# Pairing two heads' products with v on the column halves of the array, constant products at the start, and FFN steps 1.2 tiles apart

## The chip, the cores and the metric

The kernel runs on one core of a Trainium2 chip. The time is that of one execution on the device, in microseconds (us); lower is better. The engines are called TensorE (PE in the profile, with its weight loads as PEld), VectorE (DVE), ScalarE (ACT), GpSimd (POOL) and SyncE (SP, which starts the DMAs). 0.5% of this kernel's time is about 7 us.

## The reference, cut to what matters

Attention over 8 batches of 8 heads with a threshold in the softmax, and behind it a feed-forward net (FFN) over all 4608 rows:

```python
scores = scale * np.matmul(q, k.transpose(0, 1, 3, 2))          # (8, 8, 576, 576), head_dim 64
thresh = np.max(scores, axis=-1, keepdims=True) - tau
scores = np.where(scores >= thresh, scores, -1000000000.0)
scores = scores - np.max(scores, axis=-1, keepdims=True)
attn = np.exp(scores)
attn = attn / (np.sum(attn, axis=-1, keepdims=True) + 1e-09)
attn_out = np.matmul(attn, v)
...
x = attn_out.transpose(0, 2, 1, 3).reshape(4608, 512)
h = x @ w_in                                                    # 512 -> 2048
r = np.maximum(h, 0.0)
g = s * (r * r) + b
return g @ w_out                                                # 2048 -> 512
```

## The kernel before

**Tiles.** A tile is 128 queries of one head (the 64 queries left over, the tail, of two heads share a tile). For each tile (`tile_of`) PE multiplies q with k (L328, 576 scores a query in two halves of 288), DVE copies the scores out with their maximum (L331), ACT takes the exponential (L337), DVE applies the threshold and sums (L340), GpSimd divides (L348), PE transposes the weights in five pieces (L357, L358), ACT copies them out of PSUM, and PE multiplies them with v.

**The unsplit batch.** Batch 0 (`Plain`, 36 tiles) works in plain float32. Its products with v stand at L373: five for a tile (four over 128 keys and one over the last 64), each with v of 64 columns as the stationary side, so that they fill half of the array's columns. The profile counts each as two records. The transposed weights lie in `e32(i)`, one of two buffers that alternate from tile to tile; L364 and L365 copy into it, L373 reads it, and L376 copies the result out of the PSUM bank `pv` into x. A visit is one pair of heads and 256 queries; its tiles come as head 0 (two tiles, and a tail tile in some visits), then head 1 (two tiles). Batches 1 to 7 split every operand into two parts that TensorE takes faster (`Head`, L404), and their order is not touched.

**The FFN** (`Block`) works on 256 rows at a time, in 16 steps over the hidden columns: 12 products into `h` (L535), ACT and GpSimd in between, six products into `o` (L548). Before its first step a block's input is split (`stage`: ACT L518 to xh, DVE L520 to xl). Weights of step f are loaded and split on the way, in `weights`. 18 blocks of 16 steps stand against 288 tiles.

**What sets the order.** `Plan` takes every operation with its engine, cost in ns, dependencies and due time `at` (in tiles), simulates the engines and hands out the least due of what is ready. The program is then emitted in this order, and each engine works through its own queue in order. A block's step f falls due at `when + each * f`; `when` is the end of the block before, or 1.5 tiles after the tile that completes the input, whichever is later. `each` is 1.125 tiles in the first half, so that 16 steps take 18 tiles, which is the distance of two blocks.

**The start.** The first scores wait for q and k of the first pair. GpSimd fills the constants meanwhile (L673 and around it), among them `ones` (L671) and the zeros `qt` (L670).

Of the kernel before, what the change touches and what calls it, by code (L numbers as in the profile page):

```python
# [9 lines left out]
F32 = mybir.dt.float32  # L10
# [10 lines left out]
SCORES_AHEAD, VALUES_AFTER = 1, 1  # L21
FFN_AFTER = 1.5


TWO_BANKS = 16
WEIGHTS_AT, WEIGHTS_EACH = 12, 1.5
# [80 lines left out]
def tile_attention_ffn(ctx: ExitStack, tc: tile.TileContext, qT, kT, v, tau, w_in, w_out, s, b, out):  # L107
# [73 lines left out]
    def pe(n, cols, fn, r, w, at):  # L181

        plan.add("PE", (n * (0.452 * cols + 1.5), n * (0.452 * cols + 1.5) + 170), fn, r, w, at)

# [130 lines left out]
    def tile_of(ti, i):  # L315
# [4 lines left out]
        sm_k, em_k, get = buffers(i)  # L320
        plain = ti.plain

        def scores():
            for hf in range(2):
                cs = slice(hf * HS, (hf + 1) * HS)
                seq = ti.st()
                for n, (stat, kk) in enumerate(seq):
                    nc.tensor.matmul(ps[:, hf, 0:HS], stat, kk[:, cs], start=(n == 0), stop=(n == len(seq) - 1))  # L328
        pe(2 if plain else 4 * len(ti.heads), HS * (3.7 if plain else 1), scores, ti.kq(), [bk], i - SCORES_AHEAD)

# [28 lines left out]
        pe(4.3, 240, transposes, [em_k, "ident"], ["tp", "tt"], i + 0.5)  # L359
        if plain:  # L360
            ke = ("e32", i % 2)

            def both():
                nc.scalar.copy(out=e32(i)[:, 0:NQ], in_=tp)  # L364
                nc.scalar.copy(out=e32(i)[0:T, NQ], in_=tt)  # L365
            act((660, 760), both, ["tp", "tt"], [ke], i + 0.5)
            for pr, j, cs, dest, key in plain:
                n = cs.stop - cs.start

                def products(pr=pr, j=j, cs=cs, n=n):  # L370
                    for kt in range(5):
                        ks = slice(0, P if kt < NQ else T)
                        nc.tensor.matmul(bank["pv"][0:D, 0:n], pr.get()[2][ks, j, kt], e32(i)[ks, kt, cs], start=(kt == 0),  # L373
                                         stop=(kt == 4))
                pe(5, n * 4, products, [ke, pr.keys[2 + j], pr.keys[2 + j] + (1,)], ["pv"], i + VALUES_AFTER)
                act((80 + 0.75 * n, 180 + 0.75 * n), lambda dest=dest, j=j, n=n: nc.scalar.copy(  # L376
                    out=dest[j * D:(j + 1) * D], in_=bank["pv"][0:D, 0:n]), ["pv"], [key], i + VALUES_AFTER)
            return
# [210 lines left out]
    def make_tiles(vis, A, Bh):  # L589
# [7 lines left out]
        if A is Bh:  # L597
            for j in range(2):
                for i in range(2):
                    ti = Tile_()  # L600
                    c, r = t0 * P + i * P, slice(j * D, (j + 1) * D)
                    ti.st = lambda c=c, r=r: [(A.get()[1][r, c:c + P], A.get()[0][r])]
                    ti.kq = lambda: A.keys[:2]
                    ti.plain = [(A, j, fl, xb[xk][:, pair, i * P:(i + 1) * P], ("x", xk, pair, j, i))]
                    ti.heads, ti.blocks = [A], []
                    tiles.append(ti)
                if tail and not j:
# [3 lines left out]
                    ti.plain = [(A, u_, slice(u_ * T, (u_ + 1) * T), xtl, ("xt", bi % 4, pair, u_)) for u_ in range(2)]  # L611
# [50 lines left out]
    n_plain = sum(ti.plain is not None for ti in tiles)  # L662


    pairs[0].load(-30)
    dma(0.5, lambda: nc.sync.dma_start(out=tau_t, in_=tau.partition_broadcast(P)), [], ["tau"], -20)

    def constants():
        make_identity(nc, ident)
        nc.gpsimd.memset(qt.bitcast(F32), 0.0)  # L670
        nc.gpsimd.memset(ones.bitcast(F32), 1.0)  # L671
# [5 lines left out]
    pool((1500, 1500), constants, [], ["ident", "ones", "qd0", "qd1", "qt0", "qt1", "sm0", "sm1", "em0", "em1"], -9)  # L677
    for ap, t, k in (s, s_t, "s_"), (b, b_t, "b"):
# [24 lines left out]
    for i, ti in enumerate(tiles):  # L703
        ti.tag = "o" if i < TWO_BANKS and i % 2 else "s"

        events.append((i, lambda ti=ti, i=i: tile_of(ti, i)))
        for g in () if ti.plain else ti.end:
            events.append((i + 0.1, lambda g=g, i=i: with_v(g, i + VALUES_AFTER)))
        if True:
            for k_ in ti.blocks:  # L710
                when = max(when, i + FFN_AFTER)
                each = 1.125 if i < len(tiles) // 2 else 1.0

# [60 lines left out]
```

## Time and profile before

| | |
|---|---|
| median of 3 runs | 1428.97 us (1423.86 to 1429.4) |
| the profiled execution | 1427.36 us |
| its span, first to last instruction | 1425.4 us |
| mean granted clock of TensorE | 0.994 |
| first product of the first FFN block (L535) | 77.10 us after the span's start |
| first product of the second FFN block | 195.31 us |

A row of the timeline reads: start in us, length in us (of all instructions merged into the row), engine, line, operation, output <- inputs, partitions x columns of the stationary side, shape, count. A row of the groups gives count, busy us, mean ns, and the idle time ahead with what ended it. Matmuls overlap in the pipeline, so the distance of two starts says more than a length.

### The profile page before, as it was taken

The page shows a single profiled execution, that of the slowest core. Times are in us where ns is not written, and L with a number is a line of the kernel's source. Part 1 is how long each engine was busy: PE and PEld are TensorE (multiplying, and loading weights), DVE is VectorE, ACT ScalarE, POOL GpSimd, SP SyncE. Part 2 cuts the span into 40 slices and gives each one's busy share as a digit, 9 for nine tenths or more (in the row PEclk, how much of TensorE's full clock was granted, in tenths as well). Part 3 has the DMA queues.
Part 4 walks back from the last instruction along what each step waited for, and adds up shares of the span by engine and source line. Part 5 has one row for each costly group of instructions (what it writes and reads, how often), then busy time and mean ns, then how long its engine had stood idle before and what let it go on. Part 6 is the DMA issues. An engine that isn't in the chain of part 4 may idle for free.

```text
span 1425.4 us, 29320 instructions
## 1 busy us (share of the span) xinstructions
PE 1392.9 (98%) x9328; PEld 1255.2 (88%) x9328; DVE 1074.0 (75%) x3099; ACT 991.4 (70%) x2487; POOL 730.5 (51%) x798
## 2 busy tenths in 40 slices
PE   8999999999999999999999999999999999999998
PEld 5677789898898989898999999999999999999887
DVE  4877777988888887988789887888788787886101
ACT  3777667777777767777677777776777777776443
POOL 1223345656565556656566556665556556653210
PEclk9999999999999999999999999999999999999999
DMA  8610011322222221322222222222222222220000
GB/s 294 246 39 21 23 58 52 95 58 61 60 79 73 59 79 52 95 59 62 64 66 80 70 72 65 80 65 63 63 75 69 76 57 70 61 85 1 16 16 15
DMA packets 94539, 99.58 MB, mean 70 GB/s; under 512 B 34480, under 2 KB 72368, under 8 KB 94384
## 3 DMA queue, kind: packets, MB, share of 16 engines
q1 hardware_dynamic: 94384, 97.71, 23.1%
q8 instruction: 73, 1.20, 0.3%
q14 instruction: 82, 0.67, 0.1%
HBM read 88.21 MB, written 9.44 MB: 69 GB/s over the span
## 4 chain that ended last, share of the span: by engine, by line
PE 92%; DVE 5%; issue 1%; ACT 1%; POOL 0%; DMA 0%; DVEq 0%; SPq 0%; ACTq 0%; POOLq 0%
PE h L535 28%; PE o L548 27%; PE s L328 12%; PE tp L357 9%; PE pv L404 9%; PE pv L373 4%; PE tt L358 2%; DVE em L340 1%; DVE e L391 1%; PE o L328 1%; PE h L487 1%; DVE xl L520 1%; DVE oo L559 0%; DVE e L393 0%; DVE x L411 0%
## 5 line engine op out<-in xcount | busy, mean ns | idle before, releaser
L535 PE MATMUL h<-xh,w 128*128 128x256 f32 x2304 | 471.1, 287 | 2.8 <-ACT xh L518 1.7
L535 PEld LDWEIGHTS h<-xh,w 128*128 128x128 f32 x2304 | 380.9, 192 | 13.0 <-ACT g L538 3.3
L348 POOL TENSOR_SCALAR em<-em,st 128x576 f32<-128x576 f32 x288 | 251.8, 874 | 272.6 <-DVE st L345 116.5
L548 PE MATMUL o<-w,gh 128*128 128x512 f32 x1152 | 370.0, 402 | 0.9 <-ACT g L538 0.5
L542 POOL TENSOR_TENSOR gl<-g,gh 128x256 fp32r<-128x256 f32 x272 | 213.2, 784 | 276.6 <-ACT gh L541 117.7
L535 PE MATMUL h<-xl,w 128*128 128x256 f32 x1152 | 328.8, 285 | 7.3 <-DVE xl L520 7.3
L340 DVE SCALAR_TENSOR_TENSOR em<-sm,st,em 128x577 f32<-128x577 f32 x288 | 253.0, 878 | 42.1 <-ACT em L337 32.0
L331 DVE TENSOR_SCALAR_CACHE_REDUCE sm<-s 128x576 f32<-128x576 f32 x280 | 211.2, 754 | 94.3 <-PE s L328 91.8
L337 ACT ACTIVATE em<-sm,st 128x576 f32<-128x576 f32 x288 | 224.9, 781 | 33.6 <-DVE sm L331 32.6
L538 ACT ACTIVATE g<-h 128x256 f32<-128x256 f32 x288 | 109.3, 380 | 194.9 <-PE h L535 189.1
L535 PEld LDWEIGHTS h<-xl,w 128*128 128x128 f32 x1152 | 221.8, 193 | 13.4 <-DVE xl L520 8.7
L548 PE MATMUL o<-w,gl 128*128 128x512 f32 x576 | 226.3, 393 | 0.0
L548 PEld LDWEIGHTS o<-w,gh 128*128 128x128 f32 x1152 | 195.7, 189 | 25.6 <-issue 1.2
L391 DVE TENSOR_TENSOR e<-tp,e 128x512 fp32r<-128x512 f32 (+1 forms) x280 | 178.2, 636 | 50.0 <-ACT e L388 44.9
L279 POOL TENSOR_TENSOR k<-rk,k 128x576 fp32r<-128x576 f32 x112 | 169.8, 1516 | 52.8 <-ACT k L278 48.4
L388 ACT CAST e<-tp 128x512 fp32r<-128x512 f32 (+1 forms) x280 | 151.0, 539 | 63.8 <-PE tp L357 60.2
L357 PE MATMUL tp<-ident,em 128*128 128x128 f32 x1152 | 176.8, 276 | 7.7 <-DVE e L391 4.7
L328 PE MATMUL s<-k,q 128*128 128x288 f32 x896 | 166.3, 308 | 0.8 <-DVE sm L331 0.8
L357 PEld LDWEIGHTS tp<-ident,em 128*128 128x128 f32 x1152 | 138.2, 141 | 32.4 <-POOL em L348 6.2
L404 PE MATMUL pv<-e,v 128*128 128x320 f32 (+1 forms) x1008 | 154.1, 296 | 1.2 <-DVE e L391 1.2
L404 PEld LDWEIGHTS pv<-e,v 128*128 128x128 f32 x1008 | 143.2, 189 | 7.3 <-DVE e L391 2.5
L328 PEld LDWEIGHTS s<-k,q 128*128 128x128 f32 x896 | 129.7, 190 | 4.7 <-DVE sm L331 2.0
(106 smaller groups left out, 1792.2 us busy)
## 6 DMA issues: line engine op xcount, KB each, us to landing
rk<-in_k_dram SPq DMA_DIRECT2D x224, 144.0 KB, 2.8
rv<-in_v_dram SPq DMA_DIRECT2D x112, 128.0 KB, 2.1
rq<-in_q_dram SPq DMA_DIRECT2D x168, 64.0 KB, 2.2
w<-in_moe_w_in_dram SPq DMA_DIRECT2D x16, 512.0 KB, 8.6
w<-in_moe_w_out_dram SPq DMA_DIRECT2D x16, 512.0 KB, 9.0
out_dram<-oo SPq DMA_DIRECT2D x32, 256.0 KB, 2.3
rq<-in_q_dram SPq DMA_DIRECT2D x56, 80.0 KB, 2.4
rv<-in_v_dram SPq DMA_DIRECT2D x224, 16.0 KB, 2.0
```

The costliest lines, as they stand in the source:

```text
L279: pool((1420, 1450), lambda: nc.gpsimd.tensor_tensor(out=klo(), in0=rk, in1=khi().bitcast(F32), op=ALU.subtract), pk + [f"khi{j}"], [f"klo ...
L328: nc.tensor.matmul(ps[:, hf, 0:HS], stat, kk[:, cs], start=(n == 0), stop=(n == len(seq) - 1))
L331: dve((760, 840), lambda: nc.vector.tensor_scalar(out=get()[0][:, 0:S].rearrange("p (a b) -> p a b", a=2), in0=ps[:, :, 0:HS], scalar1=-SC ...
L337: act((690, 785), lambda: nc.scalar.activation(out=get()[1][:, 0:S], in_=get()[0][:, 0:S], func=AF.Exp, bias=st8[:, 0:1], scale=-1.0), [sm ...
L340: dve2((830, 930), lambda: nc.vector.scalar_tensor_tensor(out=get()[1], in0=get()[0], scalar=st8[:, 1:2], in1=get()[1], op0=ALU.is_le, op1 ...
L348: pool((800, 835), lambda: nc.gpsimd.tensor_scalar(out=get()[1][:, 0:S], in0=get()[1][:, 0:S], scalar1=st8[:, 4:5], scalar2=st8[:, 5:6], o ...
L357: nc.tensor.transpose(out=tp[:, t, :], in_=em[:, t * P:(t + 1) * P], identity=ident)
L391: dve((60 + 560 * big, 140 + 560 * big), lambda hi=hi, lo=lo, cs=cs: nc.vector.tensor_tensor(out=lo(), in0=tp[:, :, cs], in1=hi()[:, 0:NQ] ...
L404: nc.tensor.matmul(ps, g.hd.v()[:, kt, :, :], o[:, kt], start=(n == 0), stop=(n == len(seq) - 1))
L535: nc.tensor.matmul(ps, w[:, c, :], x[:, c, :], start=(i == 0), stop=(i == 3 * NC - 1))
L542: do((715, 750), lambda: eng.tensor_tensor(out=lo, in0=g, in1=hi.bitcast(F32), op=ALU.subtract), [f"g{k}", f"gh{k}"], [f"gl{k}"], at)
L548: nc.tensor.matmul(bank["o"][:, t, :], a[:, ts_], w, start=(f == 0 and i == 0), stop=(f == NF - 1 and i == 2))
```

## The change

**The pairs.** In the unsplit batch a visit's tiles now come as head 0 and head 1 of the same 128 queries, next to each other; the tail tile, where there is one, follows the first two. Head j uses buffer `e32(j)`. Only the second tile of such a pair issues products with v, for both heads: for each of the five pieces of keys, one product of head 0 into rows 0 to 63 of `pv` (column half 0 of the array) and one of head 1 into rows 64 to 127 (column half 1). One copy of 128 partitions takes both out of PSUM. The tail tile, which holds both heads anyway, does the same with its two products. The number of products stays.

**Constant products.** `keep_busy` issues products of `ones` with zeros (128x128 by 256 columns) into `h`, which nobody reads: 16 listed ahead of the first tile and 5 for each of the first five tiles, with the lowest priority, so that they stand wherever the planner's PE has nothing else. `ones` and `qt` are filled first on GpSimd for this.

**Steps and costs.** `each` is 1.2 for tiles below 100 and 1.0 behind. The planner's cost of n products is n * (0.44 * cols + 6.5) instead of n * (0.452 * cols + 1.5).

```diff
-        plan.add("PE", (n * (0.452 * cols + 1.5), n * (0.452 * cols + 1.5) + 170), fn, r, w, at)
+        plan.add("PE", (n * (0.44 * cols + 6.5), n * (0.44 * cols + 6.5) + 170), fn, r, w, at)
...
-            ke = ("e32", i % 2)
+        if unsplit:
+            ke = ("e32", ti.slot)
...
-            for pr, j, cs, dest, key in plain:
-                n = cs.stop - cs.start
-
-                def products(pr=pr, j=j, cs=cs, n=n):
+            if plain:
+
+                pr, cuts, dest, keys = plain
+                n = dest.shape[-1]
+
+                def products():
                     for kt in range(5):
                         ks = slice(0, P if kt < NQ else T)
-                        nc.tensor.matmul(bank["pv"][0:D, 0:n], pr.get()[2][ks, j, kt], e32(i)[ks, kt, cs], start=(kt == 0),
-                                         stop=(kt == 4))
-                pe(5, n * 4, products, [ke, pr.keys[2 + j], pr.keys[2 + j] + (1,)], ["pv"], i + VALUES_AFTER)
-                act((80 + 0.75 * n, 180 + 0.75 * n), lambda dest=dest, j=j, n=n: nc.scalar.copy(
-                    out=dest[j * D:(j + 1) * D], in_=bank["pv"][0:D, 0:n]), ["pv"], [key], i + VALUES_AFTER)
+                        for j, (slot, cs) in enumerate(cuts):
+                            nc.tensor.matmul(bank["pv"][j * D:(j + 1) * D, 0:n], pr.get()[2][ks, j, kt],
+                                             e32(slot)[ks, kt, cs], start=(kt == 0), stop=(kt == 4))
+                pe(5, n * 4 + 20, products, [("e32", slot) for slot, _ in cuts] + [
+                    k for x in pr.keys[2:] for k in (x, x + (1,))], ["pv"], i + VALUES_AFTER)
+                act((80 + 0.75 * n, 180 + 0.75 * n), lambda: nc.scalar.copy(out=dest, in_=bank["pv"][:, 0:n]), ["pv"], keys,
+                    i + VALUES_AFTER)
...
-            for j in range(2):
-                for i in range(2):
+            for i in range(2):
+                for j in range(2):
...
-                    ti.plain = [(A, j, fl, xb[xk][:, pair, i * P:(i + 1) * P], ("x", xk, pair, j, i))]
+                    ti.slot, ti.plain = j, j and (A, [(0, fl), (1, fl)], xb[xk][:, pair, i * P:(i + 1) * P],
+                                                  [("x", xk, pair, u_, i) for u_ in range(2)])
...
+    def keep_busy(n, r):
+
+        for _ in range(n):
+            pe(1, 2 * P, lambda: nc.tensor.matmul(bank["h"][:, 0:2 * P], ones, qt.rearrange("p j q -> p (j q)"),
+                                                 start=True, stop=True), ["ones", "qt0"] + r, ["h"], 1e6)
+    keep_busy(BUSY, [])
...
+        if i < BUSY_TILES:
+            events.append((i, lambda ti=ti: keep_busy(BUSY_EACH, [ti.tag])))
...
-                each = 1.125 if i < len(tiles) // 2 else 1.0
+                each = 1.2 if i < 100 else 1.0
```

BUSY is 16, BUSY_TILES and BUSY_EACH are 5.

**What moves on the engines.** On PE, the start of the program before (`s`, `o`: the two banks of scores; `tp`, `tt`: transposes; `x_90`, `oo`: the two buffers of `e32`; `w_107`: the first pair's operands; `em`: softmax weights):

```order
L328 MATMUL s<-w_107 128x288 x2
L328 MATMUL o<-w_107 128x288 x2
L328 MATMUL s<-w_107 128x288 x2
L328 MATMUL o<-w_107 128x288 x2
L357 MATMUL tp<-ident,em_80 128x128 x4
L358 MATMUL tt<-ident,em_80 64x128
L328 MATMUL s<-v 128x288 x2
L328 MATMUL o<-v 128x288 x2
L373 MATMUL pv<-x_90,w_107 64x128 x5
```

And the same place now (lines of the new file; L683 is a constant product):

```order
L683 MATMUL h<-qt,ones 128x256 x13
L329 MATMUL s<-w_107 128x288 x2
L329 MATMUL o<-w_107 128x288 x2
L683 MATMUL h<-qt,ones 128x256 x8
L329 MATMUL s<-w_107 128x288 x2
L683 MATMUL h<-qt,ones 128x256 x3
L358 MATMUL tp<-ident,em_80 128x128 x4
L359 MATMUL tt<-ident,em_80 64x128
L683 MATMUL h<-qt,ones 128x256 x2
L329 MATMUL o<-w_107 128x288 x2
L358 MATMUL tp<-ident,em_82 128x128 x4
L359 MATMUL tt<-ident,em_82 64x128
```

Constant products stand ahead of the first scores and between the first operations, and the second tile's transposes come ahead of any product with v, where before the next pair's scores did.

On PE, the products of a pair, here the fourth, with the second tile's transposes right ahead of them (L377 is the products' line in the new file):

```order
L358 MATMUL tp<-ident,em_82 128x128 x4
L359 MATMUL tt<-ident,em_82 64x128
L377 MATMUL pv<-x_90,v 64x128
L377 MATMUL pv<-oo,v 64x128
L377 MATMUL pv<-x_90,v 64x128
L377 MATMUL pv<-oo,v 64x128
...
```

The two heads' products alternate, and they wait for the copies of both buffers, where before five products of one buffer stood together.

On PE, the first step of the fourth FFN block, before (`xh_3615`: the new block's input; L404: products with v of a later batch; `qt`, `q_84`: its queries):

```order
L404 MATMUL pv<-e,v 128x320 x9
L357 MATMUL tp<-ident,em_80 128x128 x4
L358 MATMUL tt<-ident,em_80 64x128
L328 MATMUL s<-k,q_84 128x288 x4
L357 MATMUL tp<-ident,em_82 128x128 x4
L358 MATMUL tt<-ident,em_82 64x128
L535 MATMUL h<-xh_3615,w_320 128x256
```

And now (L409, L540 and L553 are L404, L535 and L548 of before; `xh_3591` is the new block's input, `xh_2680` the old one's):

```order
L409 MATMUL pv<-e,v 128x320 x9
L553 MATMUL o<-w_1467,gh_96 128x512 x2
L553 MATMUL o<-w_1467,gl_98 128x512
L358 MATMUL tp<-ident,em_80 128x128 x4
L359 MATMUL tt<-ident,em_80 64x128
L329 MATMUL s<-k,qt 128x288 x8
L553 MATMUL o<-w_1546,gh_95 128x512 x2
L553 MATMUL o<-w_1546,gl_97 128x512
...
L540 MATMUL h<-xh_2680,w_1619 128x256
...
L329 MATMUL s<-k,q_84 128x288 x4
L540 MATMUL h<-xh_3591,w_356 128x256
```

Before, only attention stands between the last products with v and the new block; now the last steps of the old block stand there too. Counted in tiles that are transposed ahead of them, the old block's last step and the new block's first stand at 52 and 55, 70 and 74, 88 and 91, 106 and 110, 124 and 127, 142 and 146 before, and at 53 and 56, 74 and 74, 90 and 93, 110 and 112, 128 and 129, 144 and 145 now, for the third to eighth block.

More of the change, by code (lines that the diff above doesn't have):

```diff
@@ L22 @@
 FFN_AFTER = 1.5
+BUSY, BUSY_TILES, BUSY_EACH = 16, 5, 5
 TWO_BANKS = 16
@@ L320, in tile_of @@
         sm_k, em_k, get = buffers(i)
-        plain = ti.plain
+        plain, unsplit = ti.plain, i < n_plain
         def scores():
@@ L328, in scores @@
                     nc.tensor.matmul(ps[:, hf, 0:HS], stat, kk[:, cs], start=(n == 0), stop=(n == len(seq) - 1))
-        pe(2 if plain else 4 * len(ti.heads), HS * (3.7 if plain else 1), scores, ti.kq(), [bk], i - SCORES_AHEAD)
+        pe(2 if unsplit else 4 * len(ti.heads), HS * (3.7 if unsplit else 1), scores, ti.kq(), [bk], i - SCORES_AHEAD)
         dve((760, 840), lambda: nc.vector.tensor_scalar(
@@ L359, in tile_of @@
         pe(4.3, 240, transposes, [em_k, "ident"], ["tp", "tt"], i + 0.5)
-        if plain:
-            ke = ("e32", i % 2)
+        if unsplit:
+            ke = ("e32", ti.slot)
             def both():
-                nc.scalar.copy(out=e32(i)[:, 0:NQ], in_=tp)
-                nc.scalar.copy(out=e32(i)[0:T, NQ], in_=tt)
+                nc.scalar.copy(out=e32(ti.slot)[:, 0:NQ], in_=tp)
+                nc.scalar.copy(out=e32(ti.slot)[0:T, NQ], in_=tt)
             act((660, 760), both, ["tp", "tt"], [ke], i + 0.5)
-            for pr, j, cs, dest, key in plain:
-                n = cs.stop - cs.start
-                def products(pr=pr, j=j, cs=cs, n=n):
+            if plain:
+                pr, cuts, dest, keys = plain
+                n = dest.shape[-1]
+                def products():
                     for kt in range(5):
                         ks = slice(0, P if kt < NQ else T)
-                        nc.tensor.matmul(bank["pv"][0:D, 0:n], pr.get()[2][ks, j, kt], e32(i)[ks, kt, cs], start=(kt == 0),
-                                         stop=(kt == 4))
-                pe(5, n * 4, products, [ke, pr.keys[2 + j], pr.keys[2 + j] + (1,)], ["pv"], i + VALUES_AFTER)
-                act((80 + 0.75 * n, 180 + 0.75 * n), lambda dest=dest, j=j, n=n: nc.scalar.copy(
-                    out=dest[j * D:(j + 1) * D], in_=bank["pv"][0:D, 0:n]), ["pv"], [key], i + VALUES_AFTER)
+                        for j, (slot, cs) in enumerate(cuts):
[5 more added lines that the diff above has]
+                    i + VALUES_AFTER)
             return
@@ L603, in make_tiles @@
                     ti.kq = lambda: A.keys[:2]
-                    ti.plain = [(A, j, fl, xb[xk][:, pair, i * P:(i + 1) * P], ("x", xk, pair, j, i))]
+                    ti.slot, ti.plain = j, j and (A, [(0, fl), (1, fl)], xb[xk][:, pair, i * P:(i + 1) * P],
+                                                  [("x", xk, pair, u_, i) for u_ in range(2)])
                     ti.heads, ti.blocks = [A], []
                     tiles.append(ti)
-                if tail and not j:
+                if tail and not i:
                     ti = Tile_()
@@ L610, in make_tiles @@
                     ti.kq = lambda: [A.keys[0], (f"qd{pair % 2}", 0), (f"qd{pair % 2}", 1)]
-                    ti.plain = [(A, u_, slice(u_ * T, (u_ + 1) * T), xtl, ("xt", bi % 4, pair, u_)) for u_ in range(2)]
+                    ti.slot, ti.plain = 0, (A, [(0, slice(u_ * T, (u_ + 1) * T)) for u_ in range(2)], xtl,
+                                            [("xt", bi % 4, pair, u_) for u_ in range(2)])
                     ti.heads, ti.blocks = [A], []
@@ L661, in tile_attention_ffn, with zeros @@
             tiles.append(ti)
-    n_plain = sum(ti.plain is not None for ti in tiles)
+    n_plain = sum(vis[0] == 0 for vis in visits) // 2 * 9
     pairs[0].load(-30)
     dma(0.5, lambda: nc.sync.dma_start(out=tau_t, in_=tau.partition_broadcast(P)), [], ["tau"], -20)
+    def zeros():
+        nc.gpsimd.memset(ones.bitcast(F32), 1.0)
+        nc.gpsimd.memset(qt.bitcast(F32), 0.0)
+    pool((600, 600), zeros, [], ["ones", "qt0", "qt1"], -10)
+    def keep_busy(n, r):
[3 more added lines that the diff above has]
+    keep_busy(BUSY, [])
     def constants():
         make_identity(nc, ident)
-        nc.gpsimd.memset(qt.bitcast(F32), 0.0)
-        nc.gpsimd.memset(ones.bitcast(F32), 1.0)
         for t in qd:
@@ L676, in constants @@
             nc.gpsimd.memset(c[:, S:S + 1], 1e-9)
-    pool((1500, 1500), constants, [], ["ident", "ones", "qd0", "qd1", "qt0", "qt1", "sm0", "sm1", "em0", "em1"], -9)
+    pool((900, 900), constants, [], ["ident", "qd0", "qd1", "sm0", "sm1", "em0", "em1"], -9)
     for ap, t, k in (s, s_t, "s_"), (b, b_t, "b"):
@@ L706, in tile_attention_ffn @@
         events.append((i, lambda ti=ti, i=i: tile_of(ti, i)))
-        for g in () if ti.plain else ti.end:
+        if i < BUSY_TILES:
+            events.append((i, lambda ti=ti: keep_busy(BUSY_EACH, [ti.tag])))
+        for g in () if i < n_plain else ti.end:
             events.append((i + 0.1, lambda g=g, i=i: with_v(g, i + VALUES_AFTER)))
```

## The prediction

> **What bounds the kernel now.** I read the page first (busy shares and the chain that ended last), then the busy times by stretch, then the timeline of TensorE where a stretch looked odd.
>
> ```profile
> span 1425.4 us, 29320 instructions
> PE 1392.9 (98%) x9328; PEld 1255.2 (88%) x9328; DVE 1074.0 (75%) x3099; ACT 991.4 (70%) x2487; POOL 730.5 (51%) x798
> PE 92%; DVE 5%; issue 1%; ACT 1%; POOL 0%; DMA 0%; DVEq 0%; SPq 0%; ACTq 0%; POOLq 0%
> PE h L535 28%; PE o L548 27%; PE s L328 12%; PE tp L357 9%; PE pv L404 9%; PE pv L373 4%; PE tt L358 2%; DVE em L340 1%; DVE e L391 1%; PE o L328 1%; PE h L487 1%; DVE xl L520 1%; DVE oo L559 0%; DVE e L393 0%; DVE x L411 0%
> ```
>
> TensorE (PE) makes 92% of the chain, so whatever shortens its queue or fills its holes shortens the kernel. The products that the change pairs (L373) are 4% of the span, about 57 us. The stretches show where this holds. Columns: stretch, its length, then busy us and instruction count of PE, PEld, DVE, ACT, POOL, then granted clock, DMA share, GB/s.
>
> ```profile
> 35.70:77.10 41.40, 38.59 (x237) 26.70 (x235) 34.76 (x104) 30.70 (x70) 11.26 (x12) 1.00 0.60 212
> 77.10:195.30 118.20, 118.20 (x739) 92.34 (x739) 85.77 (x224) 80.87 (x191) 41.93 (x42) 1.00 0.10 29
> 200.00:740.00 540.00, 523.58 (x3582) 484.38 (x3581) 447.72 (x1301) 394.79 (x1001) 314.87 (x337) 0.99 0.23 67
> 740.00:1300.00 560.00, 559.13 (x3909) 521.53 (x3909) 463.32 (x1356) 417.02 (x1063) 334.61 (x361) 1.00 0.24 68
> ```
>
> 77.10 us is the first product of the first feed-forward (FFN) block, 195.30 the first of the second. From 77.10 PE has no idle time. Before it, VectorE (DVE) is busy 34.76 of 41.40 us and comes second. From 200 to 740 PE is idle for 16.4 us, from 740 to 1300 for 0.9.
>
> A busy PE can still be a slow one:
>
> ```profile
> L328 PE MATMUL o<-v x8: 684/684/846, 15.3 to 28.8; 64*128 64x288 f32 x8
> L328 PE MATMUL s<-k x8: 402/403/569, 33.1 to 43.3; 64*128 64x288 f32 x8
> 17.39 2.58 PE L373 MATMUL pv<-x,w 128*64 128x128 f32 x10
> 29.37 2.58 PE L373 MATMUL pv<-x,w 128*64 128x128 f32 x10
> 31.88 1.11 PE L357 MATMUL tp<-ident,em 128*128 128x128 f32 x4
> 44.57 1.45 PE L373 MATMUL pv<-x,v 128*64 128x128 f32 x10
> 45.95 0.66 PE L357 MATMUL tp<-ident,em 128*128 128x128 f32 x4
> ```
>
> The same score product takes 684 ns until 28.8 us and 402 from 33.1 on; ten records of L373 (five products, two records each) go from 29.37 to 31.88, 2.51 us, and later from 44.57 to 45.95, 1.38. So the clock was low for the first 33 us, although the column of the granted clock says 1.00 there.
>
> **The change part by part, term 1: up to the first FFN product.** PE works without a gap from 17.39 to about 33.2 us, 15.8 us at the low clock. At the ratio 1.38/2.51 = 0.55 that work is 8.7 us: **7.1 us** to win, if 13 constant products ahead of the first scores and 8 behind them (full arrays, where the scores use half the rows and L373 half the columns) raise the clock by about 10 us. It could be nothing, if the clock waits for something else. The price of the 41: L535 has the same shape and takes 28% of 1425.4 us for 3456 products, 0.12 us each, twice that at the low clock. Thirteen lie in the idle time before the first scores; the other 28 cost 3.4 us at the full clock, of which most stand at places where PE waits for a copy or for the softmax. I charge 1 us, bounds 0 and 6.7 (28 at the low clock).
>
> The Trainium skill ("TensorE: Matmul & The Clock Gate", Part 1, What's actually happening) says that the clock is released after a busy window of about 3.4 us. By that alone it would have risen by 21 us here, from the work that starts at 17.39; the trace disagrees, with 684 ns at 28.8 us. By the rule the 7.1 would be about 1.5 us.
>
> From 35.70 to 77.10 come the products of a pair. Can two column halves run at once? No row of this trace shows column halves; the nearest are row halves:
>
> ```profile
> 6.50 1.64 PE L328 MATMUL o<-w 64*128 64x288 f32 x3
> 7.56 0.84 PE L328 MATMUL s<-w 64*128 64x288 f32 x1
> 7.94 0.68 PE L328 MATMUL o<-w 64*128 64x288 f32 x1
> 8.21 1.64 PE L328 MATMUL s<-w 64*128 64x288 f32 x3
> 9.65 1.17 PE L328 MATMUL o<-w 64*128 64x288 f32 x2
> L373 PEld LDWEIGHTS pv<-x,k x60: 129/137/138, 50.6 to 166.9; 128*64 128x64 f32 x48, 64*64 64x64 f32 x12
> ```
>
> Between o at 6.50 (head 0, lower rows) and o at 9.65 lie eight records of 0.48 us (three are (1.64 - 0.68)/2 apart): 3.84 us in a row, 3.15 measured. The first record of s (head 1, upper rows) starts at 7.56, before the last of o at 7.94: two halves did run at once. I take the same for columns. A pair then costs one group of 1.38 us, plus one record's offset of 0.11, plus about 0.1 for the short fifth step: 1.6 us instead of 2.76, **1.15 us saved a pair** (bounds 0 and 1.38). For the tail tiles:
>
> ```profile
> 88.40 0.93 PE L373 MATMUL pv<-x,w 128*64 128x64 f32 x10
> 89.26 1.23 PE L328 MATMUL s<-w 64*128 64x288 f32 x4
> 35.70:77.10 41.40, 18.84 (x132) 13.44 (x130) 1.00 0.60 212
> 77.10:195.30 118.20, 29.23 (x231) 21.34 (x230) 1.00 0.10 29
> ```
>
> A tail group is 0.86 us, two are 1.72, a pair would be some 0.95: 0.77 saved. The last two rows are the same stretches for L373 alone: 13 groups of ten records before the FFN starts, 23 behind.
>
> Thirteen groups are 6.5 pairs, 7.5 us of PE. But DVE must do its 34.76 us of work in the same stretch; at 95% busy that needs 36.6 us, so no more than **4.8 us** of it can show. There is a new wait as well. A pair's products wait for both tiles' copies out of PSUM, and where the order puts them directly behind the second tile's transposes, PE stands for the copies:
>
> ```profile
> L364 ACT COPY oo<-tp 128x512 f32<-128x512 f32 x18 | 10.5, 585 | 5.9 <-PE tp L357 5.8
> L365 ACT COPY oo<-tt 64x128 f32<-64x128 f32 x18 | 4.6, 258 | 0.0
> PE pv L373 <- ACT x L364: 1.6, 3, 0.6
> DVE em L340 <- ACT em L337: 7.0, 10, 2.0
> ```
>
> That is 0.84 us of copying, about 1.1 with the handovers, once a pair; before, the same wait came up to 0.6 us long at a few tiles (third row). Queued behind it on PE are the next tile's transposes, and DVE and GpSimd wait for those only through the next buffer. As DVE is nearly full here, the wait lies beside its work. If it did not, 6.5 x 1.1 = 7.2 us would eat this part. The fourth row is the stretch's DVE idle time: it waits for the exponentials, which come sooner when transposes release their buffer sooner. Term 1: 7.1 - 1.0 + 4.8 = **11 us**, bounds 0 and 14.6.
>
> **Term 2: 77.10 to 195.30.** 23 groups: eight tail ones and 15 full ones, 7.5 x 1.15 + 4 x 0.77 = 11.7 us of a PE that has no idle time. DVE's 85.77 us would then stand in 106 us, 81%. In this part of the order an FFN step mostly stands between the transposes and the pair's products, so the new wait is covered; I charge 1.7 for places where it is not: **10 us**, bounds 0 and 11.7. The merged copy out of PSUM (128 partitions for twice 64) takes ScalarE work away, off the chain.
>
> **Term 3: the starts of blocks, 200 to 740.** The steps of the first blocks fall due 1.2 tiles apart instead of 1.125, so 16 steps take 19.2 tiles where a block comes every 18. FFN work piles up a little, and PE has something to do while the next block's input is prepared. Today it has not:
>
> ```profile
> PE h L535 <- DVE xl L520: 5.4, 6, 1.0
> PE tp L357 <- DVE e L391: 4.7, 5, 1.5
> PE h L535 <- ACT xh L518: 1.7, 3, 0.6
> PE tp L357 <- POOL em L348: 0.5, 1, 0.5
> 510.00:524.00 14.00, 11.46 (x75) 10.46 (x74) 13.43 (x42) 9.15 (x23) 6.12 (x7) 0.88 0.31 95
> 590.00:604.00 14.00, 12.28 (x76) 10.94 (x75) 13.10 (x35) 10.03 (x25) 8.04 (x8) 0.88 0.39 118
> 670.00:688.00 18.00, 15.47 (x92) 14.20 (x91) 15.82 (x48) 12.13 (x31) 9.10 (x9) 0.81 0.33 96
> ```
>
> The first three rows are PE's longest waits from 200 to 740 (total, times, longest); the fourth is the longest from 740 to 1300, where the FFN is a block behind. The windows are three block starts: PE idle 2 us or more in each, the clock at 0.88, 0.88 and 0.81, which loses 0.12 x 14 twice and 0.19 x 18, 6.8 us together. With the 16.4 us idle that is 23 us at six starts. In the new order the fourth block's first step stands behind old steps' work instead of right behind the attention, and between the old block's last step and the new one's first lie 0, 2, 1 and 1 tiles at the fourth, sixth, seventh and eighth block, where 4, 4, 3 and 4 lay; the third and fifth keep a gap of three. DVE is full at these places (13.43 of 14), so it cannot catch up by itself. I take half: **11 us**, bounds 0 and 23. Elsewhere the new costs in the planner only trade neighbours; I take nothing.
>
> **Sum.** 11 + 10 + 11 = 32 us. The profiled execution took 1427.4 us (its span and 2 us around it), 1.6 below the median of the runs, 1428.97. 1427.4 - 32 = 1395.
>
> **The rivals.** First, the halves do not run at once, as moving data of both would pass the same rows. Then term 2 is about 0, term 1 loses its 4.8, and 6 + 11 = 17 us are left: **1410**. For it: only row halves are shown. Against: their records overlapped. The Trainium skill ("TensorE: Matmul & The Clock Gate", Part 3, The mechanism) speaks for it: a weight load overlaps running products only when their row groups differ, and both halves share the rows. The trace disagrees, since L373's loads of 137 ns fit under records 0.11 us apart on the same rows.
>
> Second, the block starts keep their waits, since DVE is full there: term 3 is 1 us, **1405**. Third, the clock stays low until 33 us; term 1 loses 7.1 and pays about 2 us more for constant products: **1404**.
>
> Fourth, on the other side: the pair's wait of 1.1 us is exposed at all 20 pairs, 22 us. It decides from (7.5 + 11.7)/20 = 0.96 us a pair on, where it eats the halves' gain; to end slower the halves must also run one after the other, and the block starts gain nothing: 1427.4 + 22 - 6 = **1443**. Against it stand the FFN steps between transposes and products.
>
> **How the numbers follow.** Forecast 0.56, first rival 0.17, second 0.14, third 0.07, fourth 0.04, and 0.02 that nothing moves. Three of the rivals lie within 15 us above the forecast; on the low side term 3 whole and term 1 at its bound give 1380. Range **1380 to 1412**. 0.5% (7 us) is about what a measurement of this kernel tells from no change: faster 0.91, same 0.05, slower 0.04.
>
> **What would show it.** Right: score products of 402 ns by 10 to 12 us; a pair's 20 records in 1.5 to 1.7 us; the first FFN product near 66 us and the second block near 174; less than 8 us of PE idle time in the six block starts. Wrong: 2.7 us for a pair; products of 684 ns past 20 us; or waits of 1 us ahead of most pairs behind the FFN's start.

## The result and the profile after

The changed kernel takes 1385.74 us (median of 4 runs, 1384.53 to 1388.92) against 1428.87 for the kernel before in the same session (1423.86 to 1429.4): a ratio of 0.9709, 95% interval 0.9682 to 0.9736, 43 us less. Forecast were 1395 us, in a range of 1380 to 1412. Executions of 1451.36 us (the kernel before), 1913.63 and 3386.68 us (one of two heads in the same column half, one of steps up to tile 144) were in the slow state, and the medians below leave them out.

The page of the changed kernel, the lines that answer to the first four of before (L540, L553, L329, L358, L409 and L377 are L535, L548, L328, L357, L404 and L373 of before; L683 is a constant product):

```profile
span 1383.6 us, 29392 instructions
PE 1356.6 (98%) x9369; PEld 1229.1 (89%) x9369; DVE 1070.8 (77%) x3099; ACT 985.9 (71%) x2467; POOL 744.7 (54%) x798
PE 91%; DVE 4%; ACT 2%; issue 1%; POOL 1%; DMA 1%; SPq 0%; DVEq 0%; ACTq 0%; POOLq 0%
PE h L540 28%; PE o L553 28%; PE s L329 12%; PE pv L409 9%; PE tp L358 9%; PE tt L359 2%; PE pv L377 2%; DVE em L341 1%; DVE sm L332 1%; PE h L492 1%; DVE e L396 0%; PE h L683 0%; DVE xl L525 0%; PE o L329 0%; ACT em L338 0%
```

The kernel is bound by the same engine as before; what was halved is the share of the unsplit products, from 4% to 2%. The busy times by stretch, columns as in the prediction:

```profile
30.00:59.30 29.30, 26.06 (x202) 17.64 (x198) 28.28 (x88) 22.68 (x51) 10.53 (x11) 1.00 1.04 363
59.30:172.90 113.60, 108.40 (x752) 83.59 (x750) 91.21 (x232) 79.97 (x186) 45.47 (x43) 0.98 0.12 34
173.00:700.00 527.00, 518.18 (x3596) 479.66 (x3595) 449.41 (x1310) 394.14 (x1002) 328.11 (x338) 1.00 0.24 70
700.00:1260.00 560.00, 559.77 (x3926) 523.49 (x3925) 457.77 (x1345) 419.74 (x1065) 333.75 (x361) 1.00 0.24 68
```

59.30 is now the first product of the first FFN block, 172.90 the first of the second. The 41.8 us of the span came from three places:

| stretch | before | after | saved | forecast |
|---|---|---|---|---|
| start to the first FFN product | 77.10 | 59.30 | 17.8 | 11 |
| to the second block's first | 118.21 | 113.60 | 4.6 | 10 |
| from there to the end | 1230.1 | 1210.7 | 19.4 | 11 |

The second row needs care. Ahead of the first landmark 17 tiles are transposed in both kernels, but between the two landmarks 20 before and 21 after. A tile took 118.21/20 = 5.91 us and takes 113.60/21 = 5.41; for the same 20 tiles that is 10.0 us saved, by this average. The one tile more then belongs to the last row, which saved 14.0.

A pair of products in the timeline of the changed kernel:

```profile
21.36 0.32 PE L377 MATMUL pv<-x,w 128*64 128x128 f32 x1
21.36 0.32 PE L377 MATMUL pv<-oo,w 128*64 128x128 f32 x1
21.52 0.27 PE L377 MATMUL pv<-x,w 128*64 128x128 f32 x1
21.52 0.27 PE L377 MATMUL pv<-oo,w 128*64 128x128 f32 x1
...
22.54 0.27 PE L377 MATMUL pv<-x,w 64*64 64x128 f32 x1
22.55 0.27 PE L377 MATMUL pv<-oo,w 64*64 64x128 f32 x1
22.75 0.38 PE L683 MATMUL h<-qt,ones 128*128 128x256 f32 x1
```

Head 0 (x) and head 1 (oo) start 0.01 us apart or less, record by record. Twenty records take 21.36 to 22.75, 1.39 us, as long as ten before (1.38). The Trainium skill ("TensorEngine Tiling (Array Packing)", Overview) gives up to twice the speed for a stationary side of 64 columns; this trace agrees, with 2 x 1.38 against 1.39.

The early clock shows in the scores of the same timeline: a record takes 0.84 us at first and 0.40 from 5.30 us on.

```profile
1.25 3.14 PE L683 MATMUL h<-qt,ones 128*128 128x256 f32 x13 [1.25 <-POOL qt L677]
4.32 0.84 PE L329 MATMUL s<-w 64*128 64x288 f32 x1
5.30 0.40 PE L329 MATMUL s<-w 64*128 64x288 f32 x1
```

### The profile page after: what moved, and what is told of

Read it like the earlier page. It is cut to its first block, busy times and chain, and to the rows that moved or that the text cites. A ratio compares the mean times of both kernels' runs of the same rounds, so it can differ in the third digit from the quotient of the medians.

```text
span 1383.6 us, 29392 instructions
## 1 busy us (share of the span) xinstructions
PE 1356.6 (98%) x9369; PEld 1229.1 (89%) x9369; DVE 1070.8 (77%) x3099; ACT 985.9 (71%) x2467; POOL 744.7 (54%) x798
## 4 chain that ended last, share of the span: by engine, by line
PE 91%; DVE 4%; ACT 2%; issue 1%; POOL 1%; DMA 1%; SPq 0%; DVEq 0%; ACTq 0%; POOLq 0%
PE h L540 28%; PE o L553 28%; PE s L329 12%; PE pv L409 9%; PE tp L358 9%; PE tt L359 2%; PE pv L377 2%; DVE em L341 1%; DVE sm L332 1%; PE h L492 1%; DVE e L396 0%; PE h L683 0%; DVE xl L525 0%; PE o L329 0%; ACT em L338 0%
## 5 line engine op out<-in xcount | busy, mean ns | idle before, releaser
L540 PE MATMUL h<-xh,w 128*128 128x256 f32 x2304 | 466.3, 285 | 4.5 <-ACT g L543 4.3
L349 POOL TENSOR_SCALAR em<-em,st 128x576 f32<-128x576 f32 x288 | 259.6, 902 | 255.0 <-DVE st L346 82.1
L540 PEld LDWEIGHTS h<-xh,w 128*128 128x128 f32 x2304 | 376.8, 190 | 15.0 <-ACT g L543 7.8
L553 PE MATMUL o<-w,gh 128*128 128x512 f32 x1152 | 369.7, 402 | 2.1 <-ACT gh L546 1.5
L547 POOL TENSOR_TENSOR gl<-g,gh 128x256 fp32r<-128x256 f32 x272 | 219.7, 808 | 254.4 <-ACT gh L546 96.2
L540 PE MATMUL h<-xl,w 128*128 128x256 f32 x1152 | 325.9, 283 | 2.3 <-DVE xl L525 2.3
L540 PEld LDWEIGHTS h<-xl,w 128*128 128x128 f32 x1152 | 219.2, 190 | 8.5 <-DVE xl L525 3.1
L553 PE MATMUL o<-w,gl 128*128 128x512 f32 x576 | 226.3, 393 | 0.3 <-POOL gl L547 0.2
L553 PEld LDWEIGHTS o<-w,gh 128*128 128x128 f32 x1152 | 196.6, 189 | 29.0 <-ACT gh L546 2.4
L358 PE MATMUL tp<-ident,em 128*128 128x128 f32 x1152 | 175.0, 274 | 5.9 <-POOL em L349 4.7
L329 PE MATMUL s<-k,q 128*128 128x288 f32 x896 | 165.9, 307 | 1.3 <-DVE sm L332 1.2
L358 PEld LDWEIGHTS tp<-ident,em 128*128 128x128 f32 x1152 | 137.2, 140 | 31.7 <-POOL em L349 8.5
L409 PE MATMUL pv<-e,v 128*128 128x320 f32 (+1 forms) x1008 | 153.0, 296 | 1.6 <-DVE e L396 1.0
L409 PEld LDWEIGHTS pv<-e,v 128*128 128x128 f32 x1008 | 141.3, 189 | 4.1 <-DVE e L396 1.4
L329 PEld LDWEIGHTS s<-k,q 128*128 128x128 f32 x896 | 129.8, 189 | 6.0 <-DVE sm L332 3.1
```

What stands on the lines that cost most here:

```text
L349: pool((800, 835), lambda: nc.gpsimd.tensor_scalar(out=get()[1][:, 0:S], in0=get()[1][:, 0:S], scalar1=st8[:, 4:5], scalar2=st8[:, 5:6], o ...
L358: nc.tensor.transpose(out=tp[:, t, :], in_=em[:, t * P:(t + 1) * P], identity=ident)
L409: nc.tensor.matmul(ps, g.hd.v()[:, kt, :, :], o[:, kt], start=(n == 0), stop=(n == len(seq) - 1))
L540: nc.tensor.matmul(ps, w[:, c, :], x[:, c, :], start=(i == 0), stop=(i == 3 * NC - 1))
L547: do((715, 750), lambda: eng.tensor_tensor(out=lo, in0=g, in1=hi.bitcast(F32), op=ALU.subtract), [f"g{k}", f"gh{k}"], [f"gl{k}"], at)
L553: nc.tensor.matmul(bank["o"][:, t, :], a[:, ts_], w, start=(f == 0 and i == 0), stop=(f == NF - 1 and i == 2))
```

## The experiments

The first product of the first FFN block is called the FFN's start below. Ratios are to the kernel before in the same session. It took 1425.9 to 1428.9 us in the four sessions, so a difference of some 3 us between kernels of different sessions tells little.

**Without constant products.**

```diff
-    keep_busy(BUSY, [])
...
-        if i < BUSY_TILES:
-            events.append((i, lambda ti=ti: keep_busy(BUSY_EACH, [ti.tag])))
```

> The changed kernel without its 41 constant products; pairs, steps and costs stay. Theory: the constants lift the clock early. Without them score products still take 684 ns past 15 us, the first FFN product comes 6 to 9 us later than the 59.3 us of the changed kernel, and the time is 1391 to 1396 us. Rival: the pairs fill the whole array and lift the clock by themselves, or the constants' own time eats what they bring: the first FFN product within 2 us of 59.3, 1384 to 1388 us.

1384.15 us (ratio to before 0.9686, 0.9629 to 0.9744), no slower than with them, and the FFN starts at 57.41 us, 1.9 earlier. The rival holds in its times, but the timeline of PE shows another reason than the two that it gives:

```profile
4.30 0.81 PE L329 MATMUL s<-w 64*128 64x288 f32 x1 [4.30 <-DMA w<-in_q_dram]
4.31 0.85 PE L329 MATMUL o<-w 64*128 64x288 f32 x1
14.41 1.12 PE L358 MATMUL tp<-ident,em 128*128 128x128 f32 x4
15.67 0.48 PE L377 MATMUL pv<-x,w 128*64 128x128 f32 x2
17.59 0.66 PE L358 MATMUL tp<-ident,em 128*128 128x128 f32 x4
```

Transposes take 1.12 us at 14.41 and 0.66 at 17.59: the clock rises at about 16 us without any constant product, when the first pair's products (15.67) have hardly begun. Ahead of them the scores of head 0 (s) and head 1 (o) start 0.01 us apart: they run at once on the two row halves, which the new order of tiles makes possible. With the constants the clock is up sooner, but not for good; in the changed kernel a transpose group is slow once more (12.80), 2.5 us behind a wait of 1.51 us. Whether that wait is the cause no run shows:

```profile
10.32 0.66 PE L358 MATMUL tp<-ident,em 128*128 128x128 f32 x4 [1.51 <-POOL em L349]
12.80 1.12 PE L358 MATMUL tp<-ident,em 128*128 128x128 f32 x4
16.74 0.60 PE L358 MATMUL tp<-ident,em 128*128 128x128 f32 x4
```

**Steps 1.125 tiles apart again.**

```diff
-                each = 1.2 if i < 100 else 1.0
+                each = 1.125 if i < len(tiles) // 2 else 1.0
```

> The changed kernel with its steps 1.125 tiles apart in the first half again. Theory: the backlog of FFN steps fills the block starts. Without it the first FFN product stays near 59 us and the second block near 173, PE's waits between 180 and 700 us rise from 7.6 us to 14 or more, the clock drops at some of the starts, and the time is 1397 to 1408 us. Rival: the waits went because of the planner's new costs or the earlier start; then 1384 to 1390 us.

1401.46 us (ratio 0.9802, 0.9743 to 0.9861), 15.7 more than the changed kernel. FFN start (59.3) and second block (173.2) stand where they stood. PE's longest waits from 180 to 700 us (total, times, longest):

```profile
PE h L540 <- DVE xl L525: 4.1, 6, 0.8
PE h L540 <- ACT g L543: 3.0, 7, 0.5
PE s L329 <- DVE sm L332: 3.0, 4, 0.9
```

The same kernel's busy times in that stretch:

```profile
173.00:700.00 527.00, 512.29 (x3520) 470.77 (x3519) 441.06 (x1286) 387.40 (x982) 310.90 (x330) 1.00 0.24 68
```

PE idles 14.7 us for 8.8 in the changed kernel, and finishes 76 products fewer in the same 527 us (3520 for 3596), which is 11 us' worth. The wait for a new block's input (the first row) is 1.9 us there in the changed kernel:

```profile
PE h L540 <- ACT g L543: 3.2, 6, 1.0
PE h L540 <- DVE xl L525: 1.9, 3, 0.8
```

The theory holds in time and place. Two parts of the expectation were wrong: the waits from 180 to 700 us come to 13.1 us and not 14, and the clock dropped at none of these block starts (1.00 in the row). Two things stay open. The first lines of its page stand against 1383.6 and 1356.6 in the changed kernel:

```profile
span 1398.7 us, 29317 instructions
PE 1365.0 (98%) x9369; PEld 1230.9 (88%) x9369; DVE 1071.7 (77%) x3099; ACT 988.9 (71%) x2467; POOL 735.1 (53%) x798
```

Of the 15.1 us that the span grew, 6.7 are idle time of PE; for the other 8.4 PE is busy longer with the same 9369 records, and no run shows why. And the edit changes two things at once: steps below tile 100 go from 1.2 tiles back to 1.125, and those of tiles 100 to 143 from 1.0 to 1.125. No run separates them.

**Both heads in the same column half.**

```diff
-                    for kt in range(5):
-                        ks = slice(0, P if kt < NQ else T)
-                        for j, (slot, cs) in enumerate(cuts):
-                            nc.tensor.matmul(bank["pv"][j * D:(j + 1) * D, 0:n], pr.get()[2][ks, j, kt],
+                    for j, (slot, cs) in enumerate(cuts):
+                        for kt in range(5):
+                            ks = slice(0, P if kt < NQ else T)
+                            nc.tensor.matmul(bank["pv"][0:D, j * n:(j + 1) * n], pr.get()[2][ks, j, kt],
...
+                    for j in range(2):
+                        nc.scalar.copy(out=dest[j * D:(j + 1) * D], in_=bank["pv"][0:D, j * n:(j + 1) * n])
```

> The changed kernel with both heads' products in column half 0, one head behind the other, into two places of the bank, and two copies out. Theory: the gain of the pairs is that the two halves run at once. Here a pair takes 2.7 us instead of 1.4. Behind the FFN's start eight full pairs and four tail pairs add 8 x 1.37 + 4 x 0.86 = 14.4 us; the eight pairs ahead of it add 3 to 9 of their 11, as VectorE covers some: 1402 to 1409 us. Rival: VectorE decides in both stretches and the halves bring little: under 8 us more, 1386 to 1393.

1404.0 us (ratio 0.9826, 0.9758 to 0.9894), 18.3 more than the changed kernel: inside the theory's range, far from the rival's. The edit also makes two copies of the one, on ScalarE. No profile of this kernel is read here.

**Two halves, one head behind the other.** The same loops turned round, but the output stays in the two column halves, with one copy.

```diff
-                    for kt in range(5):
-                        ks = slice(0, P if kt < NQ else T)
-                        for j, (slot, cs) in enumerate(cuts):
+                    for j, (slot, cs) in enumerate(cuts):
+                        for kt in range(5):
+                            ks = slice(0, P if kt < NQ else T)
```

> The changed kernel with the same two column halves, but all five products of head 0 ahead of the five of head 1. Theory: products start in the order of the program, so halves overlap only where the program alternates them: a pair takes 2.4 to 2.7 us, 1399 to 1408 us. Rival: TensorE takes the other half's product forward on its own, as it did with one score product of the other row half: a pair of 1.4 to 1.8 us, 1385 to 1390 us.

1403.07 us (ratio 0.9815, 0.9747 to 0.9884), 17.3 more. A pair in its timeline:

```profile
23.17 1.45 PE L377 MATMUL pv<-x,w 128*64 128x128 f32 x10
24.54 1.45 PE L377 MATMUL pv<-oo,w 128*64 128x128 f32 x10
25.92 0.38 PE L683 MATMUL h<-qt,ones 128*128 128x256 f32 x1
```

23.17 to 25.92 is 2.75 us: nothing overlaps but what the program alternates. The theory holds. The FFN starts at 64.2 and the second block at 190.4, with the same number of tiles between as in the changed kernel; so the overlap is worth 64.2 - 59.3 = 4.9 us ahead of the FFN and 126.2 - 113.6 = 12.6 behind its start. The second figure is rather too small: the granted clock is 1.00 there in this run and 0.98 in the changed kernel. In the run without constants, at 1.00, the same 21 tiles take 169.2 - 57.4 = 111.8 us.

**Scores kept apart, without and with constants.** A short constant product over the whole array goes ahead of each of the first 16 tiles' scores, in the kernel without constants and in the changed one.

```diff
         def scores():
+            if i < 16:
+                nc.tensor.matmul(bank["h"][:, 0:P], ones, qt[:, 0], start=True, stop=True)
             for hf in range(2):
...
```

> The changed kernel without the 41 constant products, but with one short constant product over the whole array ahead of the scores of each of the first 16 tiles, so that two heads' scores cannot run at once on the two row halves. Theory: what lifted the clock at 15.8 us without constant products is that the new order of tiles puts two heads' scores side by side. Apart, the clock stays low to 20 us or more, the first FFN product comes 5 to 10 us later than the 57.4 us of the run without constants, and the time is 1389 to 1395 us. Rival: the pairs' products lift the clock, the scores' halves are not needed; the first FFN product within 2 us of 57.4, 1383 to 1387 us.

> The changed kernel, constants and all, with the same short product between scores. Theory: here the 41 constants keep the clock up from about 5 us on, and only the overlap of scores is lost; VectorE, 96% busy from 30 us on, covers most of its 1.1 us a pair of tiles: the first FFN product 1 to 4 us behind the 59.3 us of the changed kernel, 1386 to 1390 us. Rival: the overlap itself carries the start: 6 us or more behind, 1392 us or more.

Without constants 1393.8 us (ratio 0.9782, 0.9761 to 0.9804), with them 1386.64 (0.9732, 0.9708 to 0.9756). In the first one's timeline the scores run one after the other, and the clock rises at 25 us:

```profile
4.35 2.26 PE L331 MATMUL s<-w 64*128 64x288 f32 x4 [2.63 <-DMA w<-in_q_dram]
6.94 2.29 PE L331 MATMUL o<-w 64*128 64x288 f32 x4
20.59 1.11 PE L360 MATMUL tp<-ident,em 128*128 128x128 f32 x4
21.85 0.69 PE L379 MATMUL pv<-x,w 128*64 128x128 f32 x2
24.90 0.67 PE L360 MATMUL tp<-ident,em 128*128 128x128 f32 x4
```

It rises some 3 us after the first pair's products (L379), which run on both column halves at once, have begun. The FFN's start in the four kernels:

| | scores of two heads side by side | kept apart |
|---|---|---|
| with constants | 59.3 | 60.7 |
| without | 57.4 | 66.2 |

Constants and overlapping scores do the same job. Either raises the clock early; the one makes the other needless, and without both the FFN starts 5.5 us later than with constants and 8.8 later than with overlapping scores. The 8.8 are too much for the clock alone: the short products are in the right column only, and five of them, about 0.4 us each, stand in PE's queue ahead of 18.4 us (6.53 to 6.94 is one). Where the constants hold the clock, the overlap of scores is worth at most 1.4 us, short products included. Both theories hold.

**The kernel before, with steps 1.2 tiles apart.**

```diff
-                each = 1.125 if i < len(tiles) // 2 else 1.0
+                each = 1.2 if i < 100 else 1.0
```

> The kernel before with steps 1.2 tiles apart below tile 100 and nothing else. Theory: the backlog is a gain of its own, as large as what its removal cost the changed kernel (15 us): the first FFN product stays at 77 and the second block near 195, and the time is 1411 to 1417 us. Rival: the backlog pays only together with the faster unsplit batch; then under 6 us, 1421 to 1428 us.

1416.74 us against 1425.89 of before on the same chip (ratio 0.9935, 0.9912 to 0.9959): 9 us, inside the theory's range, though short of the 15 that it names. Here too the steps of tiles 100 to 143 change, from 1.125 to 1.0. The FFN starts at 76.9 and the second block at 195.0, as before. From 200 to 740 us PE idles 13.0 us for 16.4, and the clock dips once where it dipped three times:

```profile
200.00:740.00 540.00, 527.04 (x3649) 487.94 (x3649) 460.47 (x1333) 398.87 (x1019) 336.41 (x346) 1.00 0.24 69
```

From 173 to 700 us the wait for a new block's input is nearly gone (before, it is 7.3 us at seven starts in that stretch), but a wait for softmax weights has come up:

```profile
PE tp L357 <- POOL em L348: 7.1, 5, 4.5
PE h L535 <- DVE xl L520: 0.9, 2, 0.7
```

**The changed kernel with the planner's old cost of a product.**

```diff
-        plan.add("PE", (n * (0.44 * cols + 6.5), n * (0.44 * cols + 6.5) + 170), fn, r, w, at)
+        plan.add("PE", (n * (0.452 * cols + 1.5), n * (0.452 * cols + 1.5) + 170), fn, r, w, at)
```

> The changed kernel with the planner's old cost of a product. Theory: it only trades neighbours: within 4 us of the changed kernel, 1382 to 1390 us. Rival: the new costs are a part of what the block starts gained: PE's waits from 180 to 700 us above 12 us and 1392 us or more.

1392.0 us (ratio 0.976, 0.9733 to 0.9787), 6 more than the changed kernel; the two kernels' executions do not overlap, while the intervals of their ratios just meet. The theory, within 4 us, falls, if narrowly; the rival has the time right, but PE's waits from 180 to 700 us come to 9.6 us and not to 12, and they are not those of the block starts. The longest from 173 to 700 us:

```profile
PE s L329 <- DVE sm L332: 3.4, 6, 1.8
PE tp L358 <- POOL em L349: 3.1, 5, 1.1
```

And its busy times there:

```profile
173.00:700.00 527.00, 515.63 (x3563) 476.11 (x3560) 451.44 (x1297) 391.63 (x996) 326.88 (x334) 1.00 0.25 69
```

11.4 us idle for 8.8, and 33 products fewer in the stretch. The longest waits are for scores' copies and softmax weights; that these neighbours stand too early is a reading, not shown. Of the 7.8 us between the two spans 3.6 lie further ahead, for the second block starts at 176.5 and not at 172.9, with as many tiles ahead of it.

**The kernel before with the pairs alone.** Without constants, with old costs and 1.125.

> The kernel before with the pairs alone: no constant products, the planner's old costs, steps 1.125 tiles apart. Theory: the pairs (with the scores of two heads side by side, which the new order of tiles brings) make the whole gain of the start: the first FFN product within 3 us of the 57.4 us of the run without constants, the second block near 170, and the block starts keep their waits of 12 us or more from 170 to 700 us: 1398 to 1406 us. Rival: the start needs the constants or the new costs as well; the first FFN product at 63 us or later, 1407 us or more.

1401.88 us (ratio 0.9817, 0.9771 to 0.9863). The FFN starts at 57.39 and the second block at 170.3: within about 1 us of the changed kernel without constants (57.41 and 169.2), so the start owes next to nothing to steps or costs. PE's longest waits from 173 to 700 us:

```profile
PE h L540 <- DVE xl L525: 5.4, 6, 1.0
PE tp L358 <- DVE e L396: 3.2, 4, 1.5
PE tp L358 <- POOL v L293: 3.1, 2, 1.5
```

The first is as long as in the kernel before, 5.4 us at six block starts. The theory holds: the pairs bring the start, and leave the waits of the block starts as they are.

**More backlog.** Both without constant products; the first has steps 1.3 tiles apart, the second 1.2 up to tile 144.

```diff
-                each = 1.2 if i < 100 else 1.0
+                each = 1.3 if i < 100 else 1.0
...
-                each = 1.2 if i < 100 else 1.0
+                each = 1.2 if i < 144 else 1.0
```

> The changed kernel without constant products and with steps 1.3 tiles apart below tile 100. Theory: a larger backlog fills more of the 7.9 us that PE still waits from 173 to 700 us; 2 to 6 us faster than without constants at 1.2 (1384.15): 1378 to 1382 us. Rival: what is left are waits inside steps, and fewer steps among the tiles bring VectorE to its limit: 1384 to 1392 us.

> The changed kernel without constant products and with steps 1.2 tiles apart below tile 144 instead of 100. Theory: the backlog is large enough from the fourth block on, so nothing moves: 1382 to 1387 us. Rival: a backlog that keeps growing to the eighth block fills what is left: 1378 to 1381 us.

1399.31 us (ratio 0.9796, 0.9755 to 0.9837) and 1412.47 (0.9889, 0.9846 to 0.9933): 15 and 28 us slower than 1.2 up to 100. For the first, the rival's direction holds at twice its size; for the second, both theories fall. The busy times of a stretch, of the kernel with 1.2 up to 100 and of that with 1.3:

```profile
173.00:700.00 527.00, 519.19 (x3593) 481.14 (x3594) 445.92 (x1308) 393.62 (x1002) 327.21 (x339) 1.00 0.25 69
173.00:700.00 527.00, 511.05 (x3507) 468.72 (x3508) 455.23 (x1318) 387.10 (x989) 329.75 (x333) 1.00 0.25 71
```

And a later one, of the kernel with 1.2 up to 144:

```profile
700.00:1320.00 620.00, 609.48 (x4185) 562.65 (x4184) 478.15 (x1390) 441.10 (x1124) 355.42 (x376) 0.99 0.22 62
```

The second's longest waits of PE in that stretch:

```profile
PE s L329 <- DVE sm L332: 4.0, 6, 1.5
PE o L553 <- DVE oo L564: 3.0, 2, 2.8
```

At 1.3, PE idles 16 us where 1.2 leaves 8. Up to 144, PE idles 10.5 us from 700 to 1320, where it idles 1.2 us with 1.2 up to 100, and waits for the scores' copies and for the copy that frees `o` at a block's end. A likely reading, not tested, is that PE, with FFN steps taken out of their places, runs more attention in a row and waits for VectorE. Why the second is worse than the first was not separated.

## Why the prediction was right, point by point

The direction, the order of magnitude and the three places were right; the measured time is 9 us below the forecast. Two hits are luck in part: the second block starts at 172.9 us, near the 174 of the prediction, only because the FFN starts 7 us sooner than forecast (59.3 for 66) and one tile more then stands between; and term 2 comes out at its number with other parts. By its own terms:

**The pair's price** was a little too high: 1.6 us forecast, 1.39 measured where the pair does not wait, since the second head's offset is 0.01 us instead of 0.11 and the short fifth step overlaps as well. That halves run at once was taken over from row halves, and it held. The rival that they don't is out: with the overlap taken away the kernel takes 1403 to 1404 us.

**Term 1, 17.8 us for 11**, beyond its upper bound of 14.6. The part of the products is right: 4.9 measured (halves in a row) for 4.8, and the reason fits, since VectorE is busy 28.28 of the last 29.30 us, 96.5% for the 95% that the working took. The step that failed is the one that gives the early clock to the constant products. The row halves of two heads' scores were quoted in the prediction, and the new order puts two such scores side by side, but the step never joined the two. Scores that overlap can stand in for the constants: without constants the clock rises at 16 us, and the FFN starts 1.9 us earlier than with them. So the charge of 1 us for the constants should have stood against no gain of theirs. Of the 17.8 us, 4.9 are the pair's overlap and about 5.5 the early clock (60.7 against 66.2, scores apart in both); the rest was not separated. Some of it may be that even without constants and overlapping scores the clock rises at 25 us and not at 33.

**The new wait** came ahead of the FFN's start and nowhere else. The waits of the products for the copies in the first 56 us of the changed kernel, and a pair that waits:

```profile
PE pv L377 <- ACT oo L365: 1.6, 5, 0.5
28.58 0.43 PE L377 MATMUL pv<-x,v 128*64 128x128 f32 x2
29.32 0.32 PE L377 MATMUL pv<-oo,v 128*64 128x128 f32 x1 [0.31 <-ACT oo L365]
```

The first head's product needs only the first copy and is issued at once, but the rest stands until the second copy is there: 29.32 - 28.58 = 0.74 us, of which the profile calls 0.31 idle. Six of the eight pairs ahead of the FFN's start wait so, 0.69 to 0.92 us each and 4.6 together, for the 1.1 a pair of the prediction. Behind the FFN's start the first records of both heads start 0.01 us apart in all eight full pairs, and PE's waits from 59.3 to 172.9 us hold none for these copies. So the rival on the other side, with the wait exposed at all 20 pairs, is out.

**Term 2, 10.0 us for 10**, with the same number of tiles, is right in its main part and wrong in the charge. The overlap is worth 12.6 us or rather more, by the run with halves in a row, for the 11.7 of the working. The 1.7 were charged for a wait that did not come. What is given back instead is that PE, which had no idle time here before, idles 5.2 us (113.60 - 108.40; with halves in a row 5.4), longest for the FFN's `gh` and for softmax weights, and that the granted clock is 0.98.

**Term 3, 14.0 us for 11.** That the new spacing is what brings it is shown from both sides: taking it away costs the changed kernel 15.7 us, giving it to the kernel before brings 9, and each time the wait for a new block's input goes with it (from 173 to 700 us 1.9 with it and 5.0 without; 0.9 with it and 7.3 without). That the backlog of 1.2 alone does it is not shown, for the steps behind tile 100 changed as well, from 1.125 to 1.0, and those places matter: 1.2 there costs 28 us. Nor is it shown that the clock's part of the term hangs on the spacing, for the changed kernel keeps 1.00 from 173 to 700 us with 1.125 too. The term that was mis-sized is the planner's costs, taken as nothing: with the new spacing they are worth about 6 us (1392.0 to 1385.7), part of it ahead of the second block; with 1.125 none (1401.88 with old costs, 1401.46 with new ones and constants). The rival that VectorE keeps the block starts full is out for this kernel; it may be what stops a larger backlog.

The whole, by single changes: the pairs alone take 1426.46 to 1401.88, 24.6 us; steps and costs together take that to 1384.15, 17.7 us; the constants 0, within what the runs can tell.

The Trainium skill's rule that the clock is released after a busy window of about 3.4 us ("TensorE: Matmul & The Clock Gate", Part 1, What's actually happening) fits the changed kernel, where full-array products run from 1.25 us and the scores are fast from 5.30 on. It does not fit the others: with scores apart and no constants, PE works nearly without a gap from 4.35 to 25 us, mostly on half arrays, and the clock stays low. With two halves at once from 4.30 on, it rises after about 12 us. In the kernel before, the only gap that the timeline of PE marks between 4.45 and 37 us is one of 0.23 at 12.00, so by the rule the clock would have risen sooner still than the 21 us that the prediction works out. That it counts how much of the array works is the reading that fits all four kernels; no run measured it by itself.

## What to carry to other kernels

Two products that fill half of the array each should be alternated in the program, product by product: on column halves that doubled their speed (20 records in 1.39 us for 2.75), and one behind the other gave nothing. Operations that become neighbours through a new order may overlap too, so look for them before paying for warm-up work. A backlog for the bound engine is worth having where it starves, but too much of it costs: here steps 1.2 tiles apart up to tile 100 and 1.0 behind, for 1.125 in the first half, gave 9 to 16 us, and 1.3 or 1.2 up to tile 144 took 15 and 28 away again.

## What was unexpected in the hardware

Two score products of 64 rows, on the two row halves, start 0.01 us apart and run at once; the prediction's row had shown an overlap of a record or two. And the clock of TensorE rose at 16, 25 and 33 us in three kernels (without constants; without constants and scores apart; before) whose PE was busy much alike, 9.58, 10.65 and 10.32 of the 11 us from 4 to 15: the earlier, the more of the array their products filled at once; the column of the granted clock shows 1.00 for all that time, so only the durations of equal instructions told.
